# Opening of a two-stage Fourier transform: the order of its first loads, first products and first second-stage unit

## The chip, the cores and the metric

The kernel runs on one core of one Trainium2 chip. The core has a matrix engine (TensorE, PE in the profile), VectorE (DVE), ScalarE (ACT), GpSimd (POOL) and SyncE (SP). SP and POOL also issue transfers between device memory and the core's own memory, each into a queue of its own. The metric is the device time of one execution in microseconds (us). Before the change the median of 3 runs is 673.02 us (672.89 to 673.35).

## What is computed

Two independent parts, laid side by side in the output. Part A is an attention layer with 32 heads of 18 over 2048 tokens of 576, in four segments with a running memory. Part B, the one with which the kernel begins, is a filter in the frequency domain:

```
X = rfft2(x)                     # x is 2048 x 576
X = X * (w_r + 1j * w_i)
y = irfft2(X, s=(2048, 576))
out = concatenate([attention(A_x), y], axis=-1)
```

## The kernel before

The kernel is one program for the five engines, in which the order of the instructions on each engine is the order in which the Python code writes them (the code asks for a hand-made schedule). An instruction waits until its inputs are there and until the buffer that it writes is free, and everything behind it on its engine waits with it.

**The forward transform** is the function `forward`, the first thing that runs. It works on 16 units; a unit is a block of 128 x 3 x 128 values in two mirrored halves, the input `xin`. Numbers are kept to more than the matrix engine's input precision by splitting each into a high and a low part, so that products are made three times: high by high, low by high, and high by low.

For one unit u the steps are these:

- `load(u)` fetches `xin[u]` (384 KB by the page) into one of four buffers, in SP's queue. `loadc(u)` fetches the second stage's table `cfw[u]` (384 KB) into one of three buffers, in POOL's queue.
- `prep(u)` is a generator with two halves. The first half makes sum and difference of the mirrored halves, `eo` (L126, VectorE, two instructions, two buffers), and copies their high parts `eh` on ScalarE (L129 and L130). The second half makes the low parts `el` (L133, VectorE). With `halves=True`, which the first two units have, the copies and the low parts are cut in two so that they can begin sooner.
- `f1(u)`, L145: the first stage, 14 products on TensorE (7 for each of two results) of `eh` and `el` with the tables `ftab` and `ftab2`. The table has three parts, fetched apart: `tab[:,0]`, the high part (580 KB), `tab[:,1]`, the low part (580 KB), and `tab2`, the rest (290 KB). In the order before, the seven products are: two with high input and table part 0, two with high input and table part 1, two with low input and table part 0, one with `tab2`. The result lies in one of two accumulator buffers of the tag `f1`.
- `ev0(u)`, L150, ScalarE: copies the result's high part `X0`. `ev1(u)`, L153, VectorE: the low part `X1`, after which the accumulator buffer is free again.
- `c1(u)`, L166: the second stage, 12 products on TensorE of `cfw[u]` with `X0` (eight of them) and `X1` (four), into one of two accumulators of the tag `c1`. `evz(u)`, L157, ScalarE, copies the result to `Z`, where the rest of part B works.

**Beginning.** `zeros(n)`, L172, issues n products of a tile of zeros on TensorE that nothing uses. Before the loop stand: `load(0)` in SP's queue and the first table part in POOL's; the memsets of `consts()` on POOL; the other two table parts on POOL; `load(1)`, `load(2)` and the two small constants `ident` and `bm` (L426) on SP; `loadc(0)` and `loadc(1)` on POOL; `prep` of the units 0 and 1, the first halves of both ahead of the second halves of both; `load(3)`; and 26 zeros. `f1(0)` is written in another order than the others: the four products with high input and table part 0, then 5 zeros, then the other ten.

**Loop.** Then come 20 rounds. Round u writes, among others: `ev0(u-1)`, `evz(u-3)`, the first half of `prep(u+2)`, one step of `wl`, `ev1(u-1)`, the second half of `prep(u+1)`, `f1(u)`, `load(u+4)`, `c1(u-2)`, `loadc(u+1)`. So the second stage is two units behind the first. In the rounds 0 and 1 the first half of `prep(u+2)` stands behind the second half of `prep(u+1)` instead. `wl` is the generator `load_w` for the projection weights `wqk` of part A: each step, from round 2 on, issues a load in SP's queue (L442), later steps also a copy on ScalarE (L446) and a subtraction on VectorE (L431). Attention and the inverse transform come long after.

Of the kernel before, what the change touches and what calls it, by code (L numbers as in the profile page):

```python
# [5 lines left out]
F32=mybir.dt.float32; F32R=mybir.dt.float32r  # L6
# [96 lines left out]
class FFT:  # L103
# [4 lines left out]
    def forward(s,xp,cp,pp,wl,xs,consts):  # L108

        nc,io=s.nc,s.io; v=nc.vector  # L110
        xin={}; cw={}; C={}; eh={}; el={}; F={}; X={}
        def load(u):
            xin[u]=xp.tile([128,2,3,128],F32,name="xin",bufs=4)
            nc.sync.dma_start(xin[u],io["xb"][u])
        def loadc(u):
            a,b=BORD[u]
            cw[u]=cp.tile([128,2,384],F32R,name="cfw",bufs=3)
            nc.gpsimd.dma_start(cw[u],io["cfw"][4*a+b].rearrange("p (h m) -> p h m",h=2))
        def prep(u,halves=False):

            x=xin.pop(u)
            eo=xp.tile([128,2,3,128],F32,name="eo",bufs=2)
            h=H[u%3]
            W=(slice(0,1),slice(1,2)) if halves else (slice(0,2),)
            for r,op in enumerate((OP.add,OP.subtract)):
                v.tensor_tensor(eo[:,r],x[:,0],x[:,1],op=op)  # L126
                if halves or r:
                    w=W[r] if halves else W[0]
                    nc.scalar.copy(h[:,w,:2],eo[:,w,:2])  # L129
                    nc.scalar.copy(h[64:97,w,2],eo[64:97,w,2])  # L130
            yield
            l=xp.tile([128,2,3,128],F32R,name="el",bufs=3)
            for w in W: v.tensor_tensor(l[:,w],eo[:,w],h[:,w].bitcast(F32),op=OP.subtract)  # L133
            eh[u],el[u]=h,l
            yield
        def f1(u):
            p=pp.tile([128,2,512],F32,name="f1",tag="f1")
            h,l=eh.pop(u),el.pop(u)
            L=[[(h[:,r,0],tab[:,0,r,0]),(h[:,r,1],tab[:,0,r,1]),(h[:,r,0],tab[:,1,r,0]),(h[:,r,1],tab[:,1,r,1]),
                (l[:,r,0],tab[:,0,r,0]),(l[:,r,1],tab[:,0,r,1]),(l[:99,r,2],tab2[:99,r])] for r in range(2)]  # L140
            O=[(r,n) for r in range(2) for n in range(7)]
            if u==0: O.sort(key=lambda a: a[1]>1)
            for i,(r,n) in enumerate(O):
                x,t=L[r][n]
                nc.tensor.matmul(p[:,r,:FP],x,t,start=n==0,stop=n==6)  # L145
                if u==0 and i==3: zeros(5)
            F[u]=p
        def ev0(u):
            x=xp.tile([128,2,FP],F32R,name="X0",bufs=3); X[u]=[x]
            nc.scalar.copy(x,F[u][:,:,:FP])  # L150
        def ev1(u):
            x=xp.tile([128,2,FP],F32R,name="X1",bufs=3)
            v.tensor_tensor(x,F.pop(u)[:,:,:FP],X[u][0].bitcast(F32),op=OP.subtract)  # L153
            X[u].append(x)
        def evz(u):
            a,b=BORD[u]
            nc.scalar.copy(s.Z[:,a,b],C.pop(u)[:,:,:FP])  # L157
        def c1(u):
            a,b=BORD[u]; x=X.pop(u); cc=cw.pop(u)
            p=C[u]=pp.tile([128,2,512],F32,name="c1",tag="c1")  # L160
            for r in range(2):
                n=0
                for (i,hl) in ((0,0),(0,1),(1,0)):
                    for q in range(2):
                        k=(0 if q==0 else 2) if r==0 else (1 if q==0 else 0)
                        nc.tensor.matmul(p[:,r,:FP],cc[:,hl,k*128:(k+1)*128],x[i][:,q],start=n==0,stop=n==5)  # L166
                        n+=1
        H=[xp.tile([128,2,3,128],F32R,name=f"eh{i}",bufs=1) for i in range(3)]
        z=xp.tile([128,512],BF,name="z",bufs=1)
        v.memset(z,0.0)  # L170
        def zeros(n):
            for i in range(n): nc.tensor.matmul(zp[:,0],z[:,:128],z,start=True,stop=True)  # L172
        for h in H: v.memset(h[:,:,2].bitcast(F32),0.0)
        load(0)
        tab=cp.tile([128,2,2,2,FP],F32R,name="ftab",bufs=1)
        tab2=cp.tile([128,2,FP],F32R,name="ftab2",bufs=1)
        nc.gpsimd.dma_start(tab[:,0],io["ftab"][:,:4*FP].rearrange("p (r c f) -> p r c f",r=2,c=2))
        late=consts()
        nc.gpsimd.dma_start(tab[:,1],io["ftab"][:,4*FP:].rearrange("p (r c f) -> p r c f",r=2,c=2))
        nc.gpsimd.dma_start(tab2,io["ftab2"].rearrange("p (r f) -> p r f",r=2))  # L180
        load(1); load(2); late()
        for u in range(2): loadc(u)
        p=[prep(u,True) for u in range(2)]
        for i in range(2):
            for x in p: next(x)
        p=[]
        load(3)
        zp=pp.tile([128,2,512],F32,name="f1",tag="f1")
        zeros(26)
        s.pace=Pace(44+124+32)  # L190
        for u in range(20):
            if u+2<16: p.append(prep(u+2))
            if 0<u<17: ev0(u-1)
            if 2<u<18: evz(u-3)
            if u%4==3 and u>6: s.pace.add(s.stage1((u-7)//4))
            if u>=2:
                if u<14: next(p[-1])
                next(wl,None)
            if 0<u<17: ev1(u-1)
            if 0<u<15: next(p.pop(0))  # L200
            if u<2: next(p[-1])
            if u<16: f1(u)
            if u+4<16: load(u+4)
            elif u<18: next(xs,None)
            if 1<u<18: c1(u-2)
            if u==17: evz(15)
            if 0<u<15: loadc(u+1)
            if u>13: s.pace.take(2)
        for _ in wl: pass
        for _ in xs: pass  # L210
# [5 lines left out]
    def bf(s,I,inv,turn=False,c=None):  # L216
# [5 lines left out]
        back=q[:,::-1] if c is None else q[:,:,::-1]  # L222
        L=[(t,x[0],x[2],OP.subtract,n),(q,x[1],x[3],OP.subtract,n),(x[0],x[0],x[2],OP.add,n),(x[1],x[1],x[3],OP.add,n)]
        if turn:
            o,g,h=((x[2],x[0],x[1]) if c is None else [y[:,0] for y in (x[2],x[0],x[1])])
            if inv: g,h=h,g
            L+=[(o[:,0],g[:,1],h[:,1],OP.subtract,1),(o[:,1],h[:,0],g[:,0],OP.subtract,1)]
            if c is not None: L+=[(*[y[:,1] for y in (x[2],x[0],x[1])],OP.subtract,1)]
        else: L+=[(x[2],x[0],x[1],OP.subtract,n)]
        L+=[(x[0],x[0],x[1],OP.add,n),(s.slots(p,m+1,c),t,back,OP.add,n),(s.slots(m,p+1,c),t,back,OP.subtract,n)]  # L230
        for o,a,b,op,k in L:
# [178 lines left out]
class ATT:  # L410
# [12 lines left out]
    def consts(s):  # L423
        nc,io=s.nc,s.io
        for i in range(1,4): nc.gpsimd.memset(s.zst[i],0.0)
        return lambda: (nc.sync.dma_start(s.ident,io["ident"]),nc.sync.dma_start(s.bm,io["bm"].rearrange("p (h c) -> p h c",h=7)))  # L426
# [773 lines left out]
```

## Time and profile before

| what | us |
|---|---|
| median of 3 runs | 673.02 |
| lowest and highest | 672.89, 673.35 |
| the profiled execution | 673.47 |
| its span, first to last instruction | 671.8 |
| TensorE busy | 658.6 |
| VectorE busy | 543.2 |
| ScalarE busy | 440.6 |
| GpSimd busy | 189.6 |

The durations that are used here come from one profiled execution; times in it count from the start of the span. The chain of waits starts at the last instruction and goes back from each to what released it, or to the one before on the same engine; read forward, it tells which work set the end in each stretch. The timeline shows the instructions of each engine in order of time, equal neighbours merged: start, length, engine, line, operation, output and inputs, count, and in brackets the idle time before and what ended it. PEld rows are the weight loads of TensorE, one for each product. In the DMA view q0 is POOL's queue (`software_dynamic`) and q1 is SP's (`hardware_dynamic`), with packets, MB and share of the sixteen engines in the window; an issue row ends with the time from issue to landing. The granted TensorE clock is 1.000 over the span.

### The profile page before, as it was taken

The page shows a single profiled execution, that of the slowest core. Times are in us where ns is not written, and L with a number is a line of the kernel's source. Part 1 is how long each engine was busy: PE and PEld are TensorE (multiplying, and loading weights), DVE is VectorE, ACT ScalarE, POOL GpSimd, SP SyncE. Part 2 cuts the span into 40 slices and gives each one's busy share as a digit, 9 for nine tenths or more (in the row PEclk, how much of TensorE's full clock was granted, in tenths as well). Part 3 has the DMA queues.
Part 4 walks back from the last instruction along what each step waited for, and adds up shares of the span by engine and source line. Part 5 has one row for each costly group of instructions (what it writes and reads, how often), then busy time and mean ns, then how long its engine had stood idle before and what let it go on. Part 6 is the DMA issues. An engine that isn't in the chain of part 4 may idle for free.

```text
span 671.8 us, 14143 instructions
## 1 busy us (share of the span) xinstructions
PE 658.6 (98%) x4776; PEld 484.3 (72%) x4776; DVE 543.2 (81%) x1514; ACT 440.6 (66%) x900; POOL 189.6 (28%) x387
## 2 busy tenths in 40 slices
PE   9999999999999999999999999999999999998997
PEld 5999779879879878999974454444666445663597
DVE  5998989889889778689769998998856988568643
ACT  3886796576487385444449988878756787567521
POOL 2111000100200012456506543445323564133410
PEclk9999999999999999999999999999999999999999
DMA  9896466497388478799545885876667576332152
GB/s 339 306 310 195 124 185 206 143 300 233 89 239 266 132 231 266 223 264 289 168 134 157 219 218 152 204 219 182 166 165 204 135 200 161 99 113 79 35 171 75
DMA packets 76034, 127.57 MB, mean 190 GB/s; under 512 B 12812, under 2 KB 44202, under 8 KB 72370
## 3 DMA queue, kind: packets, MB, share of 16 engines
q1 hardware_dynamic: 69310, 110.67, 57.3%
q0 software_dynamic: 5632, 15.76, 8.2%
q8 instruction: 37, 0.61, 0.4%
q10 hardware_dynamic: 1020, 0.25, 0.2%
q14 instruction: 35, 0.29, 0.1%
HBM read 81.78 MB, written 43.92 MB: 187 GB/s over the span
## 4 chain that ended last, share of the span: by engine, by line
PE 86%; DVE 5%; ACT 3%; DMA 3%; issue 2%; POOL 1%; SPq 0%; ACTq 0%; DVEq 0%; POOLq 0%
PE pj L487 15%; PE pv L763 11%; PE s L688 10%; PE pjv L487 7%; PE po L916 5%; PE i L331 4%; PE i L320 4%; PE f L145 4%; PE s L725 4%; PE c L166 4%; PE s L729 3%; PE pn L837 2%; PE s L735 2%; PE po L946 2%; PE pm L559 2%
## 5 line engine op out<-in xcount | busy, mean ns | idle before, releaser
L692 DVE CUSTOM_DVE_ANT_0 junk<-s,x 128x384 bf16<-128x384 f32 (+3 forms) x512 | 219.1, 486 | 42.2 <-PE s L688 39.7
L738 POOL TENSOR_SCALAR_AFFINE_SELECT P<-P 128x512 f32<-128x512 f32 (+2 forms) x135 | 80.6, 620 | 51.6 <-ACT P L726 47.3
L726 ACT ACTIVATE P<-s 128x512 f32<-128x512 f32 x128 | 76.7, 599 | 20.6 <-PE s L725 17.6
L763 PE MATMUL pv<-P,vs 128*32 128x512 f32 (+3 forms) x1024 | 81.0, 438 | 0.0
L731 ACT ACTIVATE P<-s 128x512 f32<-128x512 f32 x128 | 76.2, 596 | 3.4 <-PE s L730 3.0
L763 PEld LDWEIGHTS pv<-P,vs 128*32 128x32 f32 x1024 | 27.2, 109 | 44.0 <-issue 39.9
L688 PE MATMUL s<-Ks,Qs 108*128 108x512 bf16 (+3 forms) x256 | 57.7, 300 | 1.0 <-DVE mg L692 0.4
L487 PE MATMUL pj<-x,wqkh 128*128 128x512 f32 x162 | 56.1, 408 | 0.0
L232 DVE TENSOR_TENSOR Z<-Z 128x580 f32<-128x580 f32 (+2 forms) x51 | 45.9, 913 | 0.6
L692 DVE DVE_READ_ACCUMULATOR2_ANT mg<- 128x1 f32 x512 | 42.5, 83 | 0.0
L548 POOL MEMSET vt<- 128x32 f32 x16 | 2.3, 162 | 139.3 <-PE pm L559 125.5
L320 PE MATMUL i<-civ,Y 128*128 128x256 f32 (+1 forms) x288 | 39.7, 290 | 0.9 <-POOL Y L305 0.9
L736 ACT ACTIVATE P<-s 128x512 f32<-128x512 f32 x64 | 38.7, 605 | 2.5 <-PE s L735 1.1
L688 PEld LDWEIGHTS <-Qs 108*128 108x128 bf16 x320 | 26.9, 98 | 15.6 <-issue 11.0
L320 PEld LDWEIGHTS i<-civ,Y 128*128 128x128 f32 (+1 forms) x288 | 36.8, 181 | 1.9 <-POOL Y L305 1.3
L331 PE MATMUL i<-itab,T 128*128 128x290 f32 (+1 forms) x224 | 36.0, 304 | 0.1
L487 PE MATMUL pj<-x,wqkl 128*128 128x512 f32 x90 | 35.5, 395 | 0.0
L487 PE MATMUL pj<-xh,wqkh 128*128 128x512 f32 x90 | 35.5, 395 | 0.0
L487 PE MATMUL pj<-xh,wqkl 128*128 128x512 f32 x90 | 35.5, 395 | 0.0
L487 PEld LDWEIGHTS pj<-x,wqkh 128*128 128x128 f32 x162 | 30.5, 189 | 6.4
L506 DVE SCALAR_TENSOR_TENSOR ex<-pj,ex 128x512 f32<-128x512 f32 (+1 forms) x28 | 19.3, 689 | 19.5 <-ACT ex L504 19.4
L514 ACT CAST sp<-pj 128x512 bf16<-128x512 f32 x36 | 21.1, 585 | 18.6 <-DVE pj L507 18.4
(209 smaller groups left out, 1694.1 us busy)
## 6 DMA issues: line engine op xcount, KB each, us to landing
qkD<-sp SPq DMA_DIRECT2D x32, 384.0 KB
xin<-xb SPq DMA_DIRECT2D x16, 384.0 KB
cfw<-cfw POOLq DMA_DIRECT2D x16, 384.0 KB, 4.8
civ<-civ POOLq DMA_DIRECT2D x16, 384.0 KB, 8.3
Ks<-qkD SPq DMA_DIRECT2D x12, 512.0 KB
x<-qkD SPq DMA_DIRECT2D x10, 512.0 KB
Qs<-qkD SPq DMA_DIRECT2D x10, 512.0 KB
vs<-vD SPq DMA_DIRECT2D x16, 310.5 KB
```

What stands on the lines that cost most here:

```text
L232: s.nc.vector.tensor_tensor(o,a,b,op=op)
L320: nc.tensor.matmul(p[:m,k],Y[i][:,q,c*128:c*128+m],cc[:,hl,o:o+256],start=n==0,stop=n==5)
L331: nc.tensor.matmul(p,x,t,start=n==0,stop=n==6)
L487: s.nc.tensor.matmul(out,a,b,start=i==0,stop=i==len(L)-1)
L688: for o,i,e in J: nc.tensor.matmul(p[:,o:o+128*i+128],Q[:108,h+e,128*i:128*i+128],K[:108,h+e,:128*(i+1)],start=True,stop=True)
L692: nc.vector.tensor_tensor_reduce(out=junk[:,:w],in0=p[:,o:o+w],in1=s.mask[:,512-w:],scale=1.0,scalar=-3.0e38, op0=OP.add,op1=OP.max,accum_ ...
L726: nc.scalar.activation(P[0][:,hh],p0,AF.Exp,scale=SC)
L731: nc.scalar.activation(P[1][:,hh],p1,AF.Exp,scale=SC)
L736: nc.scalar.activation(P[2][:,hh-1:hh+1].rearrange("p h c -> p (h c)"),p2,AF.Exp,scale=SC)
L738: nc.gpsimd.affine_select(out=x[:,a:b],in_=x[:,a:b],pattern=[[0,b-a],[1,128]],compare_op=OP.is_ge,fill=0.0,base=0,channel_multiplier=-1)
L763: nc.tensor.matmul(s.pvt[32*hh:32*hh+32,128*j:],vt[:,152*j+19*h:152*j+19*h+32],mv[0][:,hh,mv[1]],start=j==0,stop=j>1,skip_group_check=True)
L916: nc.tensor.matmul(ps,a[t][:r,c],b[:r,t,w],start=i==0,stop=i==13)
```

## The change

Only `forward` is changed.

- `load(1)` to `load(5)` go to POOL's queue. The order on POOL is now: table part 0, `load(1)`, table part 1, `tab2`, `load(2)`, `loadc(0)`, `load(3)`, `loadc(1)`, the memsets of `consts()`, then `load(4)`, `load(5)`, `loadc(2)`. SP has `load(0)`, then `load(6)`, `ident`, `bm` and the first load of `wl`, all in round 2.
- `prep(0)` is written whole ahead of `prep(1)`.
- `f1` can issue a part of its products, and the seven are in another order: high input by table part 0, low input by table part 0, high input by table part 1, `tab2`. The first two units' products are written by parts, in turns, with 9, 4 and 4 zeros ahead of the first three parts; the 26 and 5 zeros are gone. The zeros write an accumulator of the tag `c1` now, not `f1`.
- Rounds 0 and 1 are written out ahead of the loop, which begins at 2: `ev0(0)`, first half of `prep(2)`, `ev1(0)`, second half of `prep(2)`, first half of `prep(3)`. In round 2 the first half of `prep(4)` stands behind the second half of `prep(3)`, and `c1(0)` ahead of `f1(2)`; in `c1(0)` the eight products with `X0` come first. From round 3 on the second stage is two units behind as before.

```diff
         def load(u):
             xin[u]=xp.tile([128,2,3,128],F32,name="xin",bufs=4)
-            nc.sync.dma_start(xin[u],io["xb"][u])
+            (nc.gpsimd if 0<u<6 else nc.sync).dma_start(xin[u],io["xb"][u])
...
-        def f1(u):
-            p=pp.tile([128,2,512],F32,name="f1",tag="f1")
-            h,l=eh.pop(u),el.pop(u)
-            L=[[(h[:,r,0],tab[:,0,r,0]),(h[:,r,1],tab[:,0,r,1]),(h[:,r,0],tab[:,1,r,0]),(h[:,r,1],tab[:,1,r,1]),
-                (l[:,r,0],tab[:,0,r,0]),(l[:,r,1],tab[:,0,r,1]),(l[:99,r,2],tab2[:99,r])] for r in range(2)]
-            O=[(r,n) for r in range(2) for n in range(7)]
-            if u==0: O.sort(key=lambda a: a[1]>1)
-            for i,(r,n) in enumerate(O):
-                x,t=L[r][n]
-                nc.tensor.matmul(p[:,r,:FP],x,t,start=n==0,stop=n==6)
-                if u==0 and i==3: zeros(5)
-            F[u]=p
+        def f1(u,parts=range(7)):
+            if u not in F: F[u]=pp.tile([128,2,512],F32,name="f1",tag="f1")
+            p=F[u]; h,l=eh[u],el[u]
+            L=[[(h[:,r,0],tab[:,0,r,0]),(h[:,r,1],tab[:,0,r,1]),(l[:,r,0],tab[:,0,r,0]),(l[:,r,1],tab[:,0,r,1]),
+                (h[:,r,0],tab[:,1,r,0]),(h[:,r,1],tab[:,1,r,1]),(l[:99,r,2],tab2[:99,r])] for r in range(2)]
+            for r in range(2):
+                for n in parts:
+                    x,t=L[r][n]
+                    nc.tensor.matmul(p[:,r,:FP],x,t,start=n==0,stop=n==6)
...
+            O=[(r,n) for r in range(2) for n in range(6)]
+            if u==0: O.sort(key=lambda a: a[1]>3)
+            for r,n in O:
...
-        nc.gpsimd.dma_start(tab[:,0],io["ftab"][:,:4*FP].rearrange("p (r c f) -> p r c f",r=2,c=2))
+        t4=lambda x: x.rearrange("p (r c f) -> p r c f",r=2,c=2)
+        nc.gpsimd.dma_start(tab[:,0],t4(io["ftab"][:,:4*FP]))
+        load(1)
+        nc.gpsimd.dma_start(tab[:,1],t4(io["ftab"][:,4*FP:]))
+        nc.gpsimd.dma_start(tab2,io["ftab2"].rearrange("p (r f) -> p r f",r=2))
+        load(2); loadc(0); load(3); loadc(1)
         late=consts()
-        nc.gpsimd.dma_start(tab[:,1],io["ftab"][:,4*FP:].rearrange("p (r c f) -> p r c f",r=2,c=2))
-        nc.gpsimd.dma_start(tab2,io["ftab2"].rearrange("p (r f) -> p r f",r=2))
-        load(1); load(2); late()
-        for u in range(2): loadc(u)
-        p=[prep(u,True) for u in range(2)]
-        for i in range(2):
-            for x in p: next(x)
-        p=[]
-        load(3)
-        zp=pp.tile([128,2,512],F32,name="f1",tag="f1")
-        zeros(26)
+        for u in range(2):
+            for _ in prep(u,True): pass
+        zp=pp.tile([128,2,512],F32,name="c1",tag="c1")
+        for n,u,q in ((9,0,(0,1)),(4,0,(2,3)),(4,1,(0,1)),(0,0,(4,5)),(0,1,(2,3)),(0,0,(6,)),(0,1,(4,5,6))):
+            zeros(n)
+            f1(u,q)
         s.pace=Pace(44+124+32)
-        for u in range(20):
+        ev0(0)
+        p=[prep(2),prep(3)]
+        next(p[0]); load(4)
+        ev1(0); load(5); loadc(2)
+        for _ in p.pop(0): pass
+        next(p[0])
+        for u in range(2,20):
             if u+2<16: p.append(prep(u+2))
-            if 0<u<17: ev0(u-1)
+            if u<17: ev0(u-1)
             if 2<u<18: evz(u-3)
             if u%4==3 and u>6: s.pace.add(s.stage1((u-7)//4))
-            if u>=2:
-                if u<14: next(p[-1])
-                next(wl,None)
-            if 0<u<17: ev1(u-1)
-            if 0<u<15: next(p.pop(0))
-            if u<2: next(p[-1])
+            if 2<u<14: next(p[-1])
+            if u==2: load(6); late()
+            next(wl,None)
+            if u<17: ev1(u-1)
+            if u<15: next(p.pop(0))
+            if u==2:
+                next(p[-1])
+                c1(0)
             if u<16: f1(u)
-            if u+4<16: load(u+4)
+            if u+4<16:
+                if u>2: load(u+4)
             elif u<18: next(xs,None)
-            if 1<u<18: c1(u-2)
+            if 2<u<18: c1(u-2)
             if u==17: evz(15)
-            if 0<u<15: loadc(u+1)
+            if u<15: loadc(u+1)
```

More of the change, by code (lines that the diff above doesn't have):

```diff
@@ L160, in c1 @@
             p=C[u]=pp.tile([128,2,512],F32,name="c1",tag="c1")
[L161 to L167, printed above, removed]
+            O=[(r,n) for r in range(2) for n in range(6)]
+            if u==0: O.sort(key=lambda a: a[1]>3)
+            for r,n in O:
+                i,hl=((0,0),(0,1),(1,0))[n//2]; q=n%2
+                k=(0 if q==0 else 2) if r==0 else (1 if q==0 else 0)
+                nc.tensor.matmul(p[:,r,:FP],cc[:,hl,k*128:(k+1)*128],x[i][:,q],start=n==0,stop=n==5)
         H=[xp.tile([128,2,3,128],F32R,name=f"eh{i}",bufs=1) for i in range(3)]
```

## The prediction

> **What bounds the kernel now.** The profile's first part comes first: it says which engine is hardly ever free.
>
> ```profile
> span 671.8 us, 14143 instructions
> PE 658.6 (98%) x4776; PEld 484.3 (72%) x4776; DVE 543.2 (81%) x1514; ACT 440.6 (66%) x900; POOL 189.6 (28%) x387
> ```
>
> That is TensorE, at 98%. But "busy" counts the products of zeros that only keep it running, so the next view is the chain in order of time for the first 80 us (start, length, what; x is the count).
>
> ```profile
> 1.26 8.23 PE f L172 x26
> 9.49 0.54 PE f L145 x4
> 10.04 1.09 PE f L172 x5
> 11.13 1.38 PE f L145 x10
> ...
> 19.30 1.62 PE f L145 x10
> 20.92 1.62 PE c L166 x12
> 22.54 1.90 PE f L145 x14
> ...
> 63.10 4.84 PE c L166 x36
> ```
>
> Three things are to be seen. L172, the zeros, takes 9.3 us. Between 11.13+1.38 = 12.51 us, where f1(0) ends, and 19.30 the chain is on VectorE and ScalarE. From 20.92 us on TensorE goes from unit to unit without a pause. So the edit is worth what it moves one point: the end of f1(4), now at 22.54+1.90 = 24.44 us. After it the program issues the same work in the same order, and I count a shift there one to one at the end. f1 means the 14 products of L145, c1 the 12 of L166, ev0 the copy of L150, ev1 the subtraction of L153.
>
> **The round trip.** The timeline of VectorE and ScalarE (start, busy us):
>
> ```profile
> 10.04 0.40 ACT L130 CAST eh<-eo 33x256 fp32r<-33x256 f32 x1
> 13.88 0.95 DVE L133 TENSOR_TENSOR el<-eo,eh 128x768 fp32r<-128x768 f32 x1
> 14.75 1.96 DVE L126 TENSOR_TENSOR eo<-xin 128x384 f32<-128x384 f32 x4
> 15.86 0.62 ACT L129 CAST eh<-eo 128x512 fp32r<-128x512 f32 x1 [2.69 <-DVE eo L126]
> 16.51 0.40 ACT L130 CAST eh<-eo 33x256 fp32r<-33x256 f32 x1
> 16.94 0.65 ACT L150 CAST X<-f 128x580 fp32r<-128x580 f32 x1
> 18.29 0.95 DVE L133 TENSOR_TENSOR el<-eo,eh 128x768 fp32r<-128x768 f32 x1
> 20.89 0.95 DVE L133 TENSOR_TENSOR el<-eo,eh 128x768 fp32r<-128x768 f32 x1
> ```
>
> From the start of el(2), 13.88, to that of el(3), 18.29, is 4.41 us: el, then eo(3) on VectorE, eh(3) (0.62+0.40) on ScalarE, behind it ev0(1), then ev1(1) and el(3) on VectorE. El(4) follows only 2.60 us later (20.89), because eo(4) had been done before (the four eo at 14.75) and ev0(2) had not to wait behind it.
>
> In the new order eo(4) and eh(4) stand behind el(3), and ev0(2) behind eh(4) on ScalarE. So el(3) to el(4) becomes a second trip of the same five links: el2 to el4 takes 2 x 4.41 = 8.82 us instead of 7.01, **1.81 us lost**. Of this part comes back: now f1(4) ends 24.44-21.84 = 2.60 us after el(4) does, since c1(1) stands between. In the new order f1 takes the low parts as products three and four, so 12 of 14 products follow el(4): ten took 1.62 from 19.30 with 0.06 before, two more at 1.90/14 = 0.135 make 1.95 us. That is 0.65 less. So
>
> change = (start of el(2), new) - 13.88 + 1.81 - 0.65 = (el(2), new) - 12.72.
>
> **When el(2) can start.** It follows eh(2), 1.05+0.03 us. Eh(2) needs eo(2), so xin2, and stands behind ev0(0), which needs the end of f1(0). In the old order eo(2) and eh(2) were done at 10.04+0.40 = 10.44 us, under the zeros; now they come after. Both depend on the loads, so the DMA views come next: MB of each queue (the second number) in windows of one us, from 3, 4, 5, 260, 262, 263 and 264 us on, the first table's time from issue to landing, and rows of the timeline.
>
> ```profile
> q1 hardware_dynamic: 128, 0.34, 90.7%
> ...
> q0 software_dynamic: 46, 0.21, 56.4%
> q1 hardware_dynamic: 83, 0.21, 53.3%
> ...
> q0 software_dynamic: 66, 0.30, 78.2%
> ...
> q0 software_dynamic: 13, 0.12, 77.1%
> q0 software_dynamic: 40, 0.37, 115.8%
> q0 software_dynamic: 41, 0.36, 104.0%
> q0 software_dynamic: 111, 0.28, 90.8%
> ftab<-ftab POOLq DMA_DIRECT2D x1, 580.0 KB, 6.2
> 1.31 0.72 POOL L177 DMA_DIRECT2D ftab<-ftab  x1 [0.80 <-POOLq L1187]
> 258.83 0.58 POOL L285 DMA_DIRECT2D itab<-itab  x1 [21.68 <-PE pj L487]
> 4.27 1.97 DVE L126 TENSOR_TENSOR eo<-xin 128x384 f32<-128x384 f32 x4 [2.24 <-DMA xin<-xb]
> 6.04 0.29 ACT L130 CAST eh<-eo 33x128 fp32r<-33x128 f32 x1
> ```
>
> POOL's queue (q0) moves nothing before 4 us though its first load is issued at 1.31; from then it shares with SP's (q1), 0.42 MB per us together. Alone, at 262 to 265 us, it moves 0.37, 0.36 and 0.28, mean 0.34. The first table lands at 1.31+6.2 = 7.5 us.
>
> The edit takes SP's loads out of the first 12 us (xin0 alone remains) and puts eight on POOL's queue: table 1, xin1, tables 2 and 3, xin2, cfw0, xin3, cfw1. I take 4.0 us for the first byte, 0.34 MB per us, 1.0 us from last byte to landing (an estimate: table 1, 0.594 MB, has 0.51 by 6 us, so its last byte near 6.4, and lands at 7.5). With 0.594 MB for each large table (580 KB), half for the third and 0.393 for each other load (384 KB by the page), the landings are: table 1 6.75, xin1 7.9, table 2 9.65, table 3 10.5, xin2 11.7, cfw0 12.8, xin3 14.0.
>
> TensorE's own order: 9 zeros at the early pace, then it waits.
>
> ```profile
> 5.93 0.15 PEld L172 LDWEIGHTS <-z 128*128 128x128 bf16 x1 [0.28 <-issue]
> 6.31 2.69 PEld L172 LDWEIGHTS <-z 128*128 128x128 bf16 x13 [0.23 <-issue]
> ```
>
> Until 6.3 us a zero product takes 0.15+0.28 = 0.43 us, then 2.69/13 = 0.21. Nine end at 1.26+3.84 = 5.1 us; the first table is there at 6.75. Then, at full pace: 4 products 7.33, 4 zeros 8.2, 4 products 8.7, 4 zeros 9.6. Unit 0's high parts take from 4.27 to 6.04+0.29 = 6.33, 2.06 us; with the same for unit 1, xin1's 7.9 makes 10.0, and the low parts of the second half follow 0.6 later (half of an el of 0.95, and the way to it). So f1(1)'s first four end at 10.3, f1(0)'s next 10.9, f1(1)'s low parts 11.4, f1(0)'s last two at 11.7, drained 11.85. Ev0(0) runs to 12.5; eo(2) from 11.75 to 12.8, so xin2 ends last: eh(2) from 12.85, **el(2) at 13.93**. The change is 13.93-12.72 = **+1.2 us**. In short: 14 zeros fewer, but the first products wait for loads, and f1(0)'s end, 0.7 us earlier than now (12.51), is spent on eo(2) and eh(2), which used to lie under the zeros.
>
> **What costs nothing.** Seven products by part are the same 14 per unit. C1(0) ahead of f1(2) fills a pause: f1(3) waits for el(3) at 18.3+0.95 anyway, where the old order had c1(0) at the same place. Load(4) and load(5) on POOL's queue wait for eo(0) (4.27+1.97/2 = 5.3 us) and eo(1) (near 9); behind them cfw2 and cfw3 wait, needed after 23 us. On SP, load(6) now waits for eo(2), 12.8; behind it stand ident, bm and the first wqk load, issued at 6.64 before.
>
> ```profile
> 24.32 0.68 ACT L446 CAST wqkh<-raw 128x576 fp32r<-128x576 f32 x1
> ```
>
> Its cast comes at 24.3, some 10 us after the new issue; if that cover were gone, ScalarE's queue would stop there and with it ev0. [...]
>
> **The unknowns, both ends.** The rate of POOL's queue alone: 0.28 at the lowest gives xin2 at 13.2, el(2) at 15.5, +2.75 us; 0.415, what both queues moved together, gives f1(0) drained at 11.3, el(2) at 13.1, +0.4. First byte: 4.0, or as soon after the issue as at 258.83 us (some 1.85 us, an estimate from the 0.12 MB before 261): 3.15, and el(2) at 13.1, +0.4; with both, TensorE's own list ends f1(0) at 10.9, el(2) at 12.66, -0.1. This is the floor: TensorE can't run through its 9+8 zeros and 24 products sooner. I take the rate of the three rows in which that queue is alone, as it will be.
>
> The Trainium skill, DMA: Bandwidth & Descriptors, section "Issuing engines are not separate DMA queues", says that issuing from several engines saves only the issue time, all loads running on the same sixteen engines. By that, one queue would move the 0.42 MB of two, and the sum would be +0.4. The rows of one queue alone, 0.28 to 0.37, don't bear it out here.
>
> **Rivals.**
> 1. *The fast pace comes later* (slower side). Now it comes after 5.0 us of unbroken products (1.26 to 6.3). In the new order the products break off after 3.8 us, for 1.65 us. If the pause delays the fast pace, it decides from the first product on: with it at 9.6 us, the first four take 1.0, the four zeros 1.7, f1(0) drains at 13.0, ev0(0) ends 13.7, el(2) starts at 14.8: **+2.1 us**, 675.1. Against it: 3.8 us may be enough, and no pause like this is in the profile. Chance 0.30. The Trainium skill, TensorE: Matmul & The Clock Gate, section "What's actually happening", has the clock released after a busy window of about 3.4 us that runs free of the program; nine zeros hold such a window only if it begins in the first 0.4 us of them. The one release shown here agrees in size, 5.0 us after the start; it can't show how much of a window must be busy.
> 2. *Loads come sooner* (queue at full rate, or first byte at 3.15, or both): -0.1 to +0.4, 673.2. For it: SP no longer competes. Against: the rows alone. Chance 0.20.
> 3. *POOL's queue alone near its lowest row*: +2 to +2.75, 675.4. Chance 0.10.
>
> **How the numbers follow.** The profiled execution took 673.47 us, 1.7 more than its span, and 0.45 above the median, 673.02; the change is a difference in the first 25 us and is put on the median. Forecast 673.02+1.2 = 674.2, chance 0.40, its own range 673.4 to 674.9. A measurement of this kernel tells about 0.2%, 1.35 us, from no change. Over that on the slow side: nearly all of rivals 1 and 3 and a little of the forecast, 0.42; faster by as much isn't in any case I can build (el(2) would have to start at 11.4), so 0.09 for what I don't see, out of the forecast and rival 2; the rest 0.49. The range, 672.5 to 675.9, runs from rival 2's floor less the spread of the times to rival 3.
>
> **What the profile after would show.** Zeros of L172 x17, nine of them before 5.1; a TensorE wait on the first table until 6 to 7; POOL's queue at 0.3 to 0.37 MB per us from 4 us; el(2) near 13.9, el(3) and el(4) 4.4 apart each; TensorE waiting for el before f1(3), some 2.5 us, and before f1(4), some 0.9; f1(4) ending near 25.6. Wrong if el(4) follows el(3) in under 4 us, if el(2) starts before 12.7, or if TensorE pauses again after f1(4).

## The result, and the profile after

| | median us | lowest and highest | runs |
|---|---|---|---|
| before, measured beside it | 673.18 | 672.89, 674.05 | 6 |
| after | 679.10 | 678.65, 683.07 | 6 |

The ratio is 1.0096, with a 95% interval of 1.0072 to 1.0119: the change makes the kernel slower by 5.9 us. The forecast was 674.2, in a range of 672.5 to 675.9: slower it said too, but by 1.2 us.

The profiled execution of after took 683.07 us (span 681.4), the longest of its six, against 673.47 before: 9.6 us more. So the difference of the two profiles has to be taken apart further than the 5.9 us of the medians. First the page's part on the engines, for after:

```profile
span 681.4 us, 14111 instructions
PE 661.3 (97%) x4762; PEld 487.1 (71%) x4762; DVE 543.8 (80%) x1514; ACT 440.8 (65%) x900; POOL 192.7 (28%) x392
```

TensorE issues 14 products fewer (4762 for 4776: 17 zeros in place of 31), and is busy for longer, 661.3 for 658.6. So something takes longer for each product. Where, the chain of waits of after says (start, length, what):

```profile
1.31 6.18 DMA ftab<-ftab
7.50 0.14 issue
7.63 1.31 PE f L144 x4
8.94 1.73 PE c L168 x4
10.67 0.97 PE f L144 x4
11.64 1.73 PE c L168 x4
13.37 2.09 PE f L144 x14
15.48 0.64 ACT X L147
...
17.23 0.96 DVE el L133
...
21.65 0.96 DVE el L133
...
22.65 2.32 PE f L144 x12
24.97 2.70 PE c L163 x12
27.67 1.90 PE f L144 x14
29.57 1.61 PE c L163 x12
```

L144 is f1, L168 the zeros, L163 c1. Read from above: the chain is now on the first table, where before it was on TensorE's zeros. Then come four products in 1.31 us that took 0.54 before, and four zeros in 1.73 us, 0.43 each, the early pace of the zeros before. Only from 13.37 on do 14 products take 2.09, near the 1.90 of the full pace. F1(0) is drained at 13.37+2.09 = 15.46 (before 12.51), el(2) begins at 17.23 (before 13.88), and f1(4) ends at 27.67+1.90 = 29.57 (before 24.44): 5.13 us later.

Between them stands c1(1), 24.97, with 2.70 us for 12 products that take 1.61 later. The view by windows says why (start and end, length; busy us and instructions of PE, PEld, DVE, ACT and POOL; then the granted clock, the DMA share and GB/s):

```profile
22.00:24.00 2.00, 1.67 (x11) 1.44 (x11) 2.00 (x5) 0.38 (x1) 0.00 (x0) 0.97 0.43 166
24.00:26.00 2.00, 2.00 (x11) 2.00 (x10) 1.10 (x3) 1.93 (x5) 0.00 (x0) 0.50 0.66 202
26.00:28.00 2.00, 2.00 (x12) 2.00 (x12) 1.97 (x5) 1.86 (x4) 0.03 (x1) 0.67 0.91 289
```

The clock is at a half, and by the shares missing, (0.03+0.50+0.33) x 2 / 0.5, it is so for 3.4 us, from 23.9 us on. Over 8 to 13 us, where four zeros take 1.73, the same column lists 1.00: the slow pace of the beginning doesn't show in it here and has to be read from the products, and a run's mean clock doesn't count it. This second slow stretch follows a wait of TensorE. The timeline of TensorE in after shows that wait, the one for the first table, and a third, late one (in brackets the idle time and what ended it):

```profile
7.63 1.31 PE L144 MATMUL f<-ftab,eh 128*128 128x290 f32 x4 [2.35 <-DMA ftab<-ftab]
...
21.79 0.53 PE L144 MATMUL f<-ftab,eh 128*128 128x290 f32 x2 [1.65 <-DVE X L150]
22.65 0.54 PE L144 MATMUL f<-ftab,el 128*128 128x290 f32 x2 [0.33 <-DVE el L133]
...
74.20 0.72 PE L492 MATMUL pj<-x,wqkh 128*128 128x512 f32 x2 [1.21 <-ACT Z L154]
```

The second wait is 1.65 us for ev1(1) (L150), which frees the accumulator that f1(3) writes, and 0.33 us for el(3). The timeline of before has the product that answers to the last row, the first one of the projection, pj:

```profile
67.78 0.63 PE L487 MATMUL pj<-x,wqkh 128*128 128x512 f32 x2
```

In after the first pj waits 1.21 us for the last `Z` copy of part B; before it didn't wait at all. So pj starts 74.20-67.78 = 6.42 us later, of which 5.13 come from the first 30 us and 1.21 from this wait.

What becomes of that shift? From 31 us on TensorE has the same groups of products in the same order in every kernel of this table (only inside the 14 of an f1 the order differs), and their counts differ by the zeros alone, so each can be paired with its like by counting from the end. The table gives how much later (us) a product starts than its like in the profile of before; the columns are its time there. It is worked out from the starts in the traces, for after and for seven kernels that are told of below.

| | 31 | 97 | 200 | 296 | 565 | 650 | 668 |
|---|---|---|---|---|---|---|---|
| after | 5.1 | 6.5 | 6.5 | 5.3 | 5.3 | 6.0 | 9.8 |
| e1_zeros18 | 2.1 | 3.4 | 3.4 | 2.3 | 2.3 | 2.2 | 2.0 |
| e2_zp_f1 | 3.2 | 3.0 | 3.1 | 1.8 | 2.2 | 2.6 | 4.0 |
| e5_three | 2.9 | 2.6 | 2.6 | 1.6 | 1.6 | 2.6 | 2.4 |
| e7_before_by_table | 0.3 | 0.2 | 0.1 | -0.9 | -0.9 | -1.3 | 2.4 |
| e9_before_zp_c1 | -0.4 | 1.0 | 0.9 | 2.9 | 2.9 | 3.3 | 3.1 |
| e11_late_moved | -0.6 | -0.8 | -0.8 | -1.0 | -1.0 | -0.7 | 1.3 |
| e12_fill | 1.5 | 1.2 | 1.3 | 1.6 | 1.6 | 1.9 | 1.7 |

For after, from 97 to 565 us nothing changes but for one step of -1.2 between 277 and 281 us, at a transfer. Up to 650 us 0.7 are added, and after that another 3.8, again behind a transfer. The chain of before has the two transfers so:

```profile
267.43 8.62 DMA vD<-vt
...
648.95 3.43 DMA ya<-ob
...
652.91 4.67 PE po L946 x33
```

and the chain of after so:

```profile
273.63 7.71 DMA vD<-vt
...
654.98 5.67 DMA ya<-ob
...
661.19 6.17 PE po L951 x33
```

The first is 0.91 shorter in after. The last, ya<-ob, is 2.24 longer, and after that pause of TensorE, 33 products `po` take 6.17 us for 4.67: again a stretch at half clock, by the windows of after:

```profile
662.00:664.00 2.00, 2.00 (x11) 2.00 (x11) 0.00 (x0) 0.00 (x0) 0.00 (x0) 0.55 0.59 201
664.00:666.00 2.00, 2.00 (x11) 2.00 (x10) 0.00 (x0) 0.00 (x0) 0.00 (x0) 0.60 0.00 0
```

Without 2.24 and 1.50, these 3.7 us at the end, the profiled execution would have taken 679.3, which lies among the other five (678.65 to 680.13); they left no trace, so that this alone sets it apart is not shown. The 5.3 us that stand at 565 us lie near the 5.9 of the medians.

### The profile page after: what moved, and what is told of

Same layout as the page of the kernel before. It is cut to its first block, busy times and chain, and to the rows that moved or that the text cites. A ratio compares the mean times of both kernels' runs of the same rounds, so it can differ in the third digit from the quotient of the medians.

```text
span 681.4 us, 14111 instructions
## 1 busy us (share of the span) xinstructions
PE 661.3 (97%) x4762; PEld 487.1 (71%) x4762; DVE 543.8 (80%) x1514; ACT 440.8 (65%) x900; POOL 192.7 (28%) x392
## 4 chain that ended last, share of the span: by engine, by line
PE 84%; DVE 6%; DMA 4%; ACT 3%; issue 2%; POOL 1%; ACTq 0%; SPq 0%; DVEq 0%; POOLq 0%
PE pj L492 15%; PE pv L768 10%; PE s L693 10%; PE pjv L492 8%; PE po L921 5%; PE i L336 4%; PE i L325 4%; PE f L144 4%; PE s L730 4%; PE c L163 3%; PE s L734 3%; PE po L951 2%; PE s L740 2%; PE pn L842 2%; PE pm L564 2%
```

## The experiments

Three suspects lie in the change itself: the late pace behind the wait for the first table (my rival 1), the wait of pj, which I hadn't seen coming, and the second round trip. A fourth is the move of the loads. Each kernel was run beside before on the same chip; ratios are against that, and "beside" gives before's median there.

### e1_zeros18: nine zeros more

```diff
-        for n,u,q in ((9,0,(0,1)),(4,0,(2,3)), ...
+        for n,u,q in ((18,0,(0,1)),(4,0,(2,3)), ...
```

> The changed kernel with 18 zeros ahead of the first part instead of 9, so that TensorE doesn't stop before the first table (lands at 7.5 us). Pause theory: the stop from 5.3 to 7.6 us put off the fast pace to 13.5; without it the fast pace is there by about 7, f1(0) drains near 12.0 instead of 15.5 (then bound by the low parts of unit 1 and by table 3), el(2) starts near 14.2 instead of 17.2, f1(4) ends near 26 instead of 29.6, and the median falls from 679.1 by some 3 us to about 676. Loads theory (f1(0) is late because its tables and inputs land late, whatever the pace): f1(0) still drains after 15 us and the median stays over 678.5.

Measured: 675.88 us (675.21 to 676.97, beside 673.41), ratio 1.0037 [1.0022, 1.0052]. Nine products more make the kernel 3.2 us faster than after (3.4 by the differences to before beside each). The chain:

```profile
1.26 6.42 PE c L168 x18
7.68 0.54 PE f L144 x4
8.22 0.88 PE c L168 x4
9.10 0.55 PE f L144 x4
...
10.53 1.90 PE f L144 x14
...
19.62 3.18 PE f L144 x12
```

The 18 zeros run into the first table's landing without a pause; the pace is full from the first product on (0.54 for four, 0.88 for four zeros). F1(0) is drained at 12.43 in place of 15.46, el(2) starts 1.77 later, at 14.20 in place of 17.23. That is rival 1's mechanism, shown. What remains is f1(3), whose 12 products take 3.18 us: the second slow stretch, behind a wait that the zeros don't touch. And pj still waits 1.21.

### e2_zp_f1: the zeros in an accumulator of the old tag

```diff
-        zp=pp.tile([128,2,512],F32,name="c1",tag="c1")
+        zp=pp.tile([128,2,512],F32,name="f1",tag="f1")
```

> The changed kernel with the zeros' accumulator back on the tag f1, all else as changed. Accumulator theory: which tag is used first sets which accumulator banks the two tags get, and with c1 first the first projection product takes a bank that the last evz must free; with f1 first the projections begin right behind the last c1, as before, and the median falls by 1.2 us to about 677.9; the first 30 us stay as they are. Rival (the projections wait for their inputs x, which are late): the wait of 1.2 us stays and the median stays at 679.1.

Measured: 678.92 us (677.30 to 679.86), ratio 1.0075 [1.0053, 1.0098]. The wait is gone; pj follows c1 at once:

```profile
70.89 0.62 PE L492 MATMUL pj<-x,wqkh 128*128 128x512 f32 x2
```

So the wait comes from the accumulator of the zeros: with the tag `c1`, the first pj is given one that the last copy to `Z` still reads. By which way isn't shown. The word changes two things at once: every c1 afterwards takes the other of the two accumulators than before, and `c1` is the tag that is first in use. As for the time, 1.2 us against after isn't to be told in four runs that lie 2.6 us apart.

The same chain has something else at its beginning. TensorE's work there is that of after, nine zeros, a wait for the table (2.05 us) and four products in 1.31 us from 7.33 on, but then:

```profile
10.37 0.59 PE f L144 x4
10.96 0.89 PE f L168 x4
```

The full pace was there some 3 us after the first product, not 5.7 as in after. El(2) starts at 15.91, and f1(3), behind the same wait, takes 1.90 us: this run has no second slow stretch. E3, with the same beginning, has the full pace from about 10.6 us, and el(2) at 15.54. So what the first pause costs differs from run to run, and the profile of after has a costly one.

### e3_eo4_early: the old place of eo(4)

```diff
-            if 2<u<14: next(p[-1])
+            if u<14: next(p[-1])
...
-            if u==2:
-                next(p[-1])
-                c1(0)
+            if u==2: c1(0)
```

> The changed kernel with eo(4) and eh(4) written ahead of ev1(1), as in the order before, instead of behind el(3). Round-trip theory: el(4) starts 2.6 us after el(3) instead of 4.4. The time gains less than these 1.8 us: nothing where c1(1) runs at the slow pace and ends at 27.7 anyway, up to 1.1 us where it doesn't; median 678.0 to 679.1. Rival (the second trip is set by loads or by something else in that round): el(4) still starts over 4 us after el(3).

Measured: 679.01 us (678.15 to 682.06), ratio 1.0093 [1.0063, 1.0123]. The timeline of VectorE has the third and fourth unit's low parts 2.60 us apart:

```profile
19.95 0.95 DVE L133 TENSOR_TENSOR el<-eo,eh 128x768 fp32r<-128x768 f32 x1
22.55 0.94 DVE L133 TENSOR_TENSOR el<-eo,eh 128x768 fp32r<-128x768 f32 x1
```

In after it is 26.05-21.65 = 4.40. The trip is saved, and no time is won that these runs show: f1(3) runs at the slow pace there (3.27 us), so el(4) is ready before TensorE can use it.

### e4_loads_sp: the five loads back in SP's queue

```diff
-            (nc.gpsimd if 0<u<6 else nc.sync).dma_start(xin[u],io["xb"][u])
+            nc.sync.dma_start(xin[u],io["xb"][u])
```

> The changed kernel with loads 1 to 5 back in SP's queue, at the same places in the program. Loads theory: unit 1 is there by 5.3 us and unit 2 by 8.3, so f1(0) drains 1 to 3 us sooner and the median falls to 676 to 678. Pause theory: the first table lands at 7.5 all the same, TensorE pauses as long, and from there to f1(0)'s end TensorE doesn't wait for a load but works at the slow pace; f1(0) drains within 0.5 us of 15.5 and the median stays within 0.7 us of 679.1.

Measured: 680.93 us (680.14 to 683.36), ratio 1.0114 [1.0087, 1.0141]: not faster than after. With two queues at work the inputs come sooner, but the rest of the table later. The DMA view gives the time from issue to landing of the table's third part, in after

```profile
ftab<-ftab POOLq DMA_DIRECT2D x1, 290.0 KB, 8.0
```

and in this kernel:

```profile
ftab<-ftab POOLq DMA_DIRECT2D x1, 290.0 KB, 9.2
```

In the profile f1(0) is drained at 14.27 us and f1(4) ends at 28.36, each 1.2 before that of after. Here the granted clock shows the beginning: it is 1.00 until 8 us, 0.67, 0.50, 0.50 and 0.62 in the four windows of one us from 8 to 12, and 1.00 again from 12 on. The first four products, at 7.63, take 0.78 us. So in this run the nine zeros had brought the full pace, and it was lost for 3.4 us behind the pause. The lead doesn't reach the end, where ya<-ob takes 5.19 us and 33 `po` 6.16. As the clock counts the slow beginning here and not in after, the means of the two kernels (0.992 to 0.997, 0.995 to 1.000) can't be compared. These runs give no sign that the move into GpSimd's queue costs time; e6 below asks it again without the pause.

### e5_three and e10_z18_zp: the causes together

e10 has the edits of e1 and e2, e5 those of e1, e2 and e3; the loads stay in GpSimd's queue.

> The changed kernel with 18 zeros first and the zeros on the tag f1, but eo(4) and eh(4) behind el(3) as changed: with the 18 zeros alone (675.9) and all three (673.8) it shows how the 2 us between them divide. Accumulator theory: 1.2 us below the 18 zeros alone, some 674.7, and the second round trip has the other 0.9. Rival (the round trip has it all): 675.9.

> The changed kernel with three parts undone or mended at once: 18 zeros first, zeros on the tag f1, eo(4) and eh(4) ahead of ev1(1). The loads stay in POOL's queue. If these three are the whole loss: f1(0) drains near 12.4 and el(2) starts near 14.2 as with 18 zeros alone, el(4) near 21.2 instead of 23.0, no wait ahead of the projections; f1(4) ends at 25.0 to 26.5 by whether f1(3) falls into the slow pace again, and the median is 0 to 1.3 us above the kernel before. If a fourth cause of over a microsecond lies elsewhere, it is 2 us or more above.

| kernel | edits undone | median us (runs) | beside | ratio |
|---|---|---|---|---|
| after | none | 679.10 (6) | 673.18 | 1.0096 [1.0072, 1.0119] |
| e1_zeros18 | pause | 675.88 (6) | 673.41 | 1.0037 [1.0022, 1.0052] |
| e10_z18_zp | pause, accumulator | 674.82 (10) | 673.33 | 1.0013 [1.0002, 1.0024] |
| e5_three | pause, accumulator, second trip | 673.82 (10) | 673.30 | 1.0007 [0.9994, 1.0020] |

By the differences to "beside", 5.9, 2.5, 1.5 and 0.5 us, the pause is worth 3.4, the accumulator 1.0, the second trip 1.0; half a microsecond is left, within what can be measured. The three account for the loss. Of the steps only the pause is clear of the intervals; those of e1 and e10 touch, and those of e10 and e5 overlap (among the runs with a mean clock of 0.999 or more, seven of e10 have a median of 674.66 and five of e5 673.13). That they add up in this order doesn't say that each would bring as much alone; e2 and e3 show that they don't.

### e6_three_sp: e5 with the five loads in SP's queue

The edit of e4 on e5.

> The same three, and loads 1 to 5 back in SP's queue: what the loads' queue is worth once the pace is fast. Loads theory (units 1 and 2 land 3 us sooner, so f1(0) drains sooner): 1 us or more faster than the three alone. Rival: the tables then share the engines with SP's loads, the third lands at 12.3 instead of 10.8 as in the run with SP's queue alone, f1(0) waits for it and drains near 12.8, and this is 0 to 0.7 us slower than the three alone.

Measured: 675.48 us (673.02 to 676.57), ratio 1.0036 [1.0022, 1.0051], 1.7 us above e5's median. So no run shows the move of the loads to be a loss. Nor is it shown to be a gain: the one run of e6 at a mean granted clock of 0.999 took 673.02, as e5's do at that clock, and the three others have 0.997 (see the next kernel).

### e12_fill: zeros in the wait ahead of f1(3)

e5, and ten products of zeros into the accumulator that c1(1) will use, at the place where TensorE waits for ev1(1) and el(3).

```diff
+            if u==3:
+                C[1]=pp.tile([128,2,512],F32,name="c1",tag="c1")
+                for i in range(10): nc.tensor.matmul(C[1][:,0],z[:,:128],z,start=True,stop=True)
```

> The changed kernel with the three parts mended, and ten zeros into c1(1)'s accumulator ahead of f1(3), where TensorE waits some 2.5 us for el(3). Pause theory: the wait before f1(3) makes the slow pace of 3.4 us that follows in most runs; filled, f1(3) takes 1.9 us instead of 3.2 and the median falls by 0.5 to 1.3 us below the 673.8 of the three alone, to about the kernel before. Rival (the slow pace comes from the first pause or by chance): f1(3) is as slow as often, and the median stays.

Measured: 674.75 us (673.39 to 677.56), ratio 1.0019 [1.0007, 1.0030]. The same window of e5

```profile
22.00:24.00 2.00, 2.00 (x10) 2.00 (x10) 1.97 (x4) 0.91 (x3) 0.00 (x0) 0.51 1.04 396
```

and of e12:

```profile
22.00:24.00 2.00, 2.00 (x17) 2.00 (x16) 1.97 (x5) 1.24 (x3) 0.00 (x0) 1.00 1.02 384
```

The slow stretch is gone, f1(3) takes 1.90 us in place of 3.16. The median is not lower. For each run its mean granted clock is on record, and that tells more: a stretch of 3.4 us at half lowers the mean over 672 us by 0.0025. Of e5's ten runs five have a clock of 0.999 or 1.000, and took 672.53 to 673.55 us; five have 0.996 or 0.997, and took 674.09 to 675.67. By their clock half of e5's runs have such a stretch and half have none, 2 us apart, though the program is the same in all. The profiled run, 675.67 us, is one of those with it. Of e12's twelve runs eleven are at 0.999 or above, yet they took 673.39 to 675.46: more than e5's undisturbed ones. The fill does what it should to the clock. In the profiled run it is 1.3 us ahead of e5's at 200 us, by the table of shifts, and has nothing left of that at 296, behind a transfer that took 7.91 us in e5's chain:

```profile
268.57 9.10 DMA vD<-vt
```

For the other runs it is open why they aren't as quick as e5's. The 23 runs of before measured beside e12 are all at 0.999 or 1.000 and took 672.18 to 675.70, so the clock isn't all that scatters.

### e7, e8 and e11: parts of the change put on the kernel before

e7_before_by_table writes the first two units' products by table part in the kernel before, with 18 zeros ahead of them for its 31.

```diff
-        zeros(26)
+        zeros(18)
+        for u,q in ((0,(0,1)),(0,(2,3)),(1,(0,1)),(1,(2,3)),(0,(4,5)),(0,(6,)),(1,(4,5,6))): f1(u,q)
...
-            if u<16: f1(u)
+            if 1<u<16: f1(u)
```

> The kernel before with one part of the change alone: the first two units' products by table part, with 18 zeros ahead and none between; loads, queues, order of VectorE and ScalarE and the accumulators' tags as before. Expected by the landings of before (table parts 7.5, 9.2, 11.0, unit 1 by 5.3): f1(0) drains near 11.4 instead of 12.5, el(2) starts near 12.8, f1(4) ends near 23.4 instead of 24.4; median 0.7 to 1.1 us below the kernel before. Rival (VectorE's round trip sets f1(4), and the low parts as third and fourth products wait for it longer): no gain, within 0.4 us.

Measured: 675.39 us (672.64 to 677.93), ratio 1.0023 [1.0009, 1.0037]. Fewer zeros win nothing, because the third part of the table, issued late in the old order, now ends the chain, and f1(0) is drained at 12.55 as before (12.51). By the table of shifts it is 0.9 us ahead of before at 565 us, and 2.4 behind at the end. Its chain, in the beginning and at the end:

```profile
3.09 8.86 DMA ftab<-ftab
...
647.70 5.51 DMA ya<-ob
...
653.75 6.18 PE po L944 x33
```

So the profiled run, 675.82 us, lost its lead at the place at which that of after lost time: ya<-ob took 5.51 us, and the `po` behind it ran at the slow pace. The twelve runs divide by their clock: four at 0.999 or 1.000 took 672.64 to 674.06, as before does, and eight at 0.994 to 0.997 took 675.07 to 677.93.

e8_before_prep_early adds to e7 the first half of `prep(3)` ahead of `ev0(0)`, so that the second round trip goes the short way.

```diff
+            if u<2: next(p[-1])
             if 0<u<17: ev0(u-1)
...
-            if u<2: next(p[-1])
```

> The same as the kernel before by table, and the first half of prep(3) written ahead of ev0(0) instead of behind el(2), so that ev0(1) no longer stands behind eh(3). Round-trip theory: el(3) starts some 2.6 us after el(2) instead of 4.4, TensorE doesn't wait from the second unit on, f1(4) ends near 22.4; median 1.5 to 2.2 us below the kernel before, which would beat both. Rival (xin3 lands after 11 us and holds eo(3), eh(3) and with it ev0(0) up): no faster than by table alone.

Measured: 679.20 us (676.79 to 680.26), ratio 1.0079 [1.0063, 1.0094]. Slower by 5.9 us, though by the timeline el(3) follows el(2) after 2.60 us: eh(3) now stands ahead of ev0(0) in ScalarE's queue, and waits for xin3, which is issued behind the small loads `ident` and `bm` in SP's queue and lands at 12.85. TensorE waits 4.12 us for it, and runs at half clock for 6.8 us after that, by granted clocks of 0.84, 0.50 and 0.81 in the windows of four us from 12 to 24. The mean clock is 0.995 in all six runs.

e11_late_moved issues `ident` and `bm` in round 2 instead, as the change does.

```diff
-        load(1); load(2); late()
+        load(1); load(2)
...
+                if u==2: late()
                 next(wl,None)
```

> The kernel before by table with prep(3) early, and ident and bm loaded in round 2 instead of ahead of load(3). Queue theory: the 512-byte rows of ident and bm, taken in turns with POOL's long ones, held xin3 to 12.9 us; without them xin3 lands near 10, eo(3) and eh(3) are done before f1(0) drains near 11.5 to 12, TensorE has no wait over a microsecond from f1(2) on, f1(4) ends near 23, and the median is 0.5 to 1.5 us below the kernel before. Rival (the queues share all there is, xin3 is late because of the 3 MB ahead of it): xin3 lands after 12 and the median stays over the kernel before by 3 us or more.

Measured: 676.77 us (674.77 to 677.53), ratio 1.0045 [1.0029, 1.0060]. The wait for xin3 in the chain of e8:

```profile
3.20 9.65 DMA xin<-xb
```

The same in the chain of e11, with its transfer at the end:

```profile
2.19 8.06 DMA xin<-xb
...
648.22 5.48 DMA ya<-ob
```

Xin3 lands at 10.25 in place of 12.85: issued 1.01 earlier, and 1.59 us quicker on the way. F1(4) ends at 23.84, 0.6 ahead of before, and the lead is 1.0 at 565 us by the table. Then ya<-ob takes 5.48 us, where before's profile has 3.43, and the lead is gone. The median is 3.4 us above before's, more than the profiled run, 674.77, shows. The profiled one is the only one of the six with a clock of 1.000; the five others have 0.995 to 0.997, so one or two slow stretches each by the working under e12, and where these lie isn't shown. No run here tests the transfers at the end by themselves.

### e9_before_zp_c1: the accumulator alone, in the kernel before

```diff
-        zp=pp.tile([128,2,512],F32,name="f1",tag="f1")
+        zp=pp.tile([128,2,512],F32,name="c1",tag="c1")
         zeros(26)
```

> The kernel before with one word changed: the zeros' accumulator has the tag c1, so that this tag is the first in use. Accumulator theory: the first projection product waits 1.2 us for the last evz, as in the changed kernel, and the median rises by 1.2 us, to 1.0014 to 1.0022 of the kernel before; the first 65 us stay as they are. Rival (the wait is taken up by slack further on): the wait shows in the profile and the median doesn't move.

Measured: 675.97 us (675.05 to 676.60, beside 673.33), ratio 1.0035 [1.0023, 1.0048].

The timeline of TensorE:

```profile
68.77 0.73 PE L487 MATMUL pj<-x,wqkh 128*128 128x512 f32 x2 [1.22 <-ACT Z L157]
```

and one of the windows:

```profile
282.00:284.00 2.00, 2.00 (x12) 2.00 (x11) 0.21 (x2) 0.76 (x2) 1.90 (x4) 0.51 0.84 233
```

One word brings the wait of 1.22 us into a kernel that has nothing else of the change: that is shown. But the loss is 2.6 us. In the profiled run the rest is vD<-vt (9.29 us there) and a slow stretch at 282 us behind it. Four of the six runs have a clock of 1.000, and took 675.05 to 676.27 all the same, so that stretch isn't the whole of the rest, and it stays open.

## Why the prediction was wrong, and where it was right

**The direction: right, mostly for reasons that the sum didn't have.** The second trip, which it had, is some 1.0 of the 5.9 us; the pause and the accumulator, which it had at nothing, are the rest.

**The end of f1(4) is what counts: held in part.** 5.1 us at 31 us are 5.3 at 565, with +1.4 and -1.2 between them. "One to one at the end" needs more care than I took: a transfer behind which TensorE waits anyway can give a microsecond back or take two, as the table shows for e7 and e11. And the prediction's own sign of being wrong, that TensorE pauses again after f1(4), came true: it did ahead of pj.

**The second round trip: held.** From el(2) to el(3) and on to el(4) I said 4.41 each. After has the first two at 17.23 and 21.65 in its chain, and the third in VectorE's timeline, so 4.42 and 4.40:

```profile
26.05 0.95 DVE L133 TENSOR_TENSOR el<-eo,eh 128x768 fp32r<-128x768 f32 x1
```

Its net price was put at 1.81-0.65 = 1.16 us, and e10 less e5 gives 1.0; as their intervals overlap, that is no proof of the size.

**The start of el(2), 13.93: this step failed.** It came at 17.23, 3.30 us late, because f1(0) was drained at 15.46 and not at 11.85. Term by term: the first product came at 7.63 for 6.75 (+0.88, of which the table's landing is 0.75). The first four products took 1.31 for 0.58, the four zeros 1.73 for 0.87, the next four products 0.97 for 0.50, the next zeros 1.73 for 0.90: +2.89 in all. The last 14 took 2.09 for 2.25 (-0.16). The sum is 3.61; the rest came back because xin2, landing at 12.0, did not end last as I had it. So "then, at full pace" is the sentence that was wrong. I had held the pause for a rival, with chance 0.30, and had bounded it wrongly: I let the fast pace come at 9.6 us, on no row, and it came near 13.4. In this run the 9 zeros and the 2.35 us of idle time behind them counted for nothing: from the first product at 7.63 it took again some 5.7 us, longer than the 5.0 of before, until the pace was full. Had rival 1 been priced with the 5.0 us that the profile of before gives, counted from the first product after the pause, it would have said 11.8 and some 3 us (an estimate), not 2.1. Other profiles with the same nine zeros have it less late: el(2) at 15.91 in e2, 15.54 in e3 and 16.03 in e4, so 1.6 to 2.1 us behind the 13.93, and not 3.30. With 18 zeros it is 14.20, 15.01, 14.11 and 15.06 (e1, e5, e10, e12). So the step is the same in all, its size is not. E1 shows the price by the medians: 3.4 us of the loss.

The Trainium skill, TensorE: Matmul & The Clock Gate, section "What's actually happening", has this clock released after a busy window and throttled after an idle one, windows of 3413 ns that run free of the kernel. The stretches of 3.4 us in the windows agree with that length, and that e5 has one in half of its runs agrees with windows that begin anywhere, as do the different beginnings of after, e2, e3 and e4. Its idle window of about 3.4 us the trace doesn't bear out: 1.65 and 0.33 us of idle time were enough ahead of 23.9 us.

**The pause before f1(3): seen, not priced.** I expected "TensorE waiting for el before f1(3), some 2.5 us" and gave it no price beyond the wait. Most of it was for something else: 1.65 us for ev1(1), which frees the accumulator, and 0.33 for el(3). It was the cause of the second slow stretch, since with the wait filled eleven of e12's twelve runs have the full clock, against five of e5's ten. In after, f1(4) came 29.57-27.01 = 2.56 us after the end of el(4), not 1.95, so 0.61 us here; in e5 one such stretch costs 2 us. With the real start of el(2), 17.23, the prediction's formula gives 4.51 us, and with these 0.61 it is the 5.13 that f1(4) came late.

**"The zeros write an accumulator of the tag c1": not followed.** It stands in the description of the change, and the prediction gave it no term. The price is a wait of 1.2 us at the first pj (e2 and e9), about 1.0 of the loss by e1 and e10; in the kernel before the same word cost 2.6 (e9), of which the rest is open.

**The loads: a loss that the runs don't show.** I had the first products wait for the loads in GpSimd's queue, since the bytes would go at 0.34 MB per us. MB of that queue (second number) in the windows 4 to 5, 8 to 9 and 10 to 11 us of after:

```profile
q0 software_dynamic: 71, 0.32, 97.7%
...
q0 software_dynamic: 141, 0.40, 113.7%
...
q0 software_dynamic: 129, 0.43, 116.8%
```

The first table landed later than I said (7.5 for 6.75), then the queue alone moved as much as both had together. The second table landed at 2.57+7.7 = 10.3 (I said 9.65), the third at 11.1 (10.5), xin2 at 12.0 (11.7): near, but by luck, as a first landing put too early and a rate put too low nearly cancel. And with the loads on SP neither e4 nor e6 came out faster. The Trainium skill, DMA: Bandwidth & Descriptors, section "Issuing engines are not separate DMA queues", says that all loads run on the same sixteen engines, whoever issues them; from 8 us on the trace agrees, with 0.40 to 0.43 MB per us by one queue against 0.42 by two. I had set that against rows of 0.28 to 0.37 from another stage and taken the rows.

## What to carry to other kernels

Products of zeros that only keep TensorE running are worth their time when they reach without a gap to the first real product: here nine of them taken away cost 3.4 us. Price a pause of TensorE at the pause and up to a whole new slow start behind it (here 3 to 5.7 us from the first product on), and expect that price to differ from run to run. Which tag a throw-away accumulator has can change which later tile waits, however far down the program it stands: here at 70 us, for a tile taken at 1 us.

## What the runs showed of the hardware that was not expected

- TensorE's half clock comes in stretches of 3.4 us (22 to 28, 662 to 666 us in after, 282 to 286 in e9) or twice that (e8), after waits of TensorE. These can be short: 1.65 and 0.33 us in after, 0.29, 0.65 and 0.27 us in e9. The same wait has one in after's profile and none in e2's. The same kernel has one in some runs and not in others: e5 took 672.53 to 673.55 us without, 674.09 to 675.67 with.
- GpSimd's queue by itself moved 0.30 to 0.34 MB per us between 4 and 8 us, and 0.40 to 0.43 from 8 to 14 us (after).
- Two small loads (64 and 65.5 KB) ahead of a load of 384 KB in one queue can hold it up: with them moved away it was issued 1.01 us earlier and landed 2.60 earlier (one profile each of e8 and e11).
- The transfers ya<-ob and vD<-vt, far from the change, took 3.43 to 5.67 and 7.50 to 9.29 us from one profile to another. In the profiles of e7, e11 and e12 a lead of about 1 us was lost behind one of them.
